# Second products of odd token tiles moved to the last stage of an attention and feed-forward kernel

## The chip, the cores and the metric

The kernel runs on one core of a Trainium2 chip. The metric is the device time of one execution in microseconds. TensorE (PE) multiplies matrices into PSUM banks; VectorE (DVE) and ScalarE (ACT) empty the banks and do element-wise work; GpSimd (POOL) does some sums and issues some DMAs; SyncE (SP) issues the other DMAs. Each engine takes its instructions in order.

## The reference

Eight batches, 12 heads, 448 positions, head width 64; the model width is 12 x 64 = 768, and the hidden width of the feed-forward part is 3072.

```python
def _attn_ref(q, k, v):
    S = q.shape[2]
    scale = 1.0 / np.sqrt(q.shape[-1])
    scores = scale * np.matmul(q, k.transpose(0, 1, 3, 2))
    attn = np.maximum(scores, 0.0) ** 2 / S
    return np.matmul(attn, v).astype(np.float32)

def _moe_ref(x, g_ln, w_ch1, w_ch2):      # x: attention's output, (8, 448, 768)
    mu = np.mean(x, axis=-1, keepdims=True)
    var = np.mean((x - mu) ** 2, axis=-1, keepdims=True)
    xn = (x - mu) / np.sqrt(var + 1e-06) * g_ln
    ch = np.maximum(xn @ w_ch1, 0.0) @ w_ch2
    return (x + ch).astype(np.float32)
```

The inputs are float32; the matrix products run in bf16 with float32 sums.

## The kernel before, in words

**Pairs and stages.** Two batches make a pair: 896 tokens, seven token tiles of 128. There are four pairs, 0 to 3. For each pair the kernel computes attention, the first product with `w_ch1` and ReLU (FFN1, into the tile `hT`, 24 row blocks of 128 hidden units by 896 tokens), and the second product with `w_ch2` (FFN2). The order on PE is written out by hand. After the first pair's start it goes: FFN2 of pair 0 with attention of pair 1 woven in, FFN1 of pair 1, FFN2 of pair 1 with attention of pair 2, FFN1 of pair 2, FFN2 of pair 2 with attention of pair 3, FFN1 of pair 3, FFN2 of pair 3 alone. The last of these is called the last stage.

**The weave.** `interleave` spreads a list of attention units over a list of FFN2 units. An attention unit is mostly a *bundle* of three score tiles (`item`, `scores`): four small matmuls on PE each (L366), a ReLU on ACT (L377) from PSUM into `attn_sb`, and a square, either on DVE (L381) or on ACT (L379). In the second and fourth pair's attention ACT squares the third tile of every bundle. A bundle may also hold a value product (`values`, 28 matmuls, L398), evicted by DVE into `xT` (L404). Score tiles and value products share a ring of three PSUM buffers of two banks each (`ps_sc`). At the last score tile of a group, `transposed` starts the key and query transposes of a later group on SP (L313, L318, L319); inputs are loaded from POOL (L159).

**FFN2 of pairs 0 and 1.** `ffn2_units` goes token tile by token tile: two column halves of 24 matmuls (128x128 by 128x384), each cut in four units of six. `finish` (L756) scales the result by the token's `rstd`, adds the residual from `xt_room` (`xtok`), and `store` sends it out on SP through one of three buffers in `o_room` (L776). Pair 1 leaves out its middle tile, `MID` = 3: `odd_out` (L789) sends that tile's 24 blocks of `hT` and its residual rows to DRAM, and its `rstd` column is kept in `odd_root`. In pair 0's stage `fold_beside` also folds the layer norm's gain and mean into `w1` on DVE (L485).

**FFN2 of pairs 2 and 3: Strassen.** `ffn2_pair` takes two token tiles at once (t and t+4). Two tiles, two halves of the hidden width and two column halves make a 2x2 by 2x2 block product, done with seven products of twelve matmuls in the place of eight. It needs sums of blocks of `hT` (`h_sums_of`, on DVE) and of `w_ch2` (`w2_sum_units`, done earlier), and sums of banks (`z`, L1130 to L1184). Pair 2 does three such pairs and its middle tile by `ffn2_mid` (48 matmuls, L1076). Pair 3 does four; the fourth is its own middle tile with the one that pair 1 sent out, read back by `odd_in` (L795) into parts of `w1` that are free by then. With `third`, `ffn2_pair` starts with products 4, 3 and 1 and puts off their last block of rows, so that the last FFN1 block (`close`) can end between them.

**FFN1 of pairs 1 to 3** is a Strassen scheme too (L903), whose weight sums are made on POOL and DVE in pair 1 (L864 to L888), kept in DRAM and read back.

Of the kernel before, what the change touches and what calls it, by code (L numbers as in the profile page):

```python
# [28 lines left out]
def kernel(  # L29
# [22 lines left out]
    nc = tc.nc  # L52
    P = 128
# [13 lines left out]
    K2 = d_ff // P  # L67
# [27 lines left out]
    odd_root = const.tile([P, 1], fp32)  # L95
# [162 lines left out]
    def transposes(b, m):  # L258
# [11 lines left out]
        if (b, m) == (0, 0):  # L270
# [5 lines left out]
            idle(32)  # L276
# [323 lines left out]
    def attention(bs, hooks):  # L600
# [25 lines left out]
        def bundle(items, at):  # L626
            for o, it in enumerate(items):
                item(*it, o == 2 and bs[0] in (by_dma, B - 2))
                if o == at:
                    product(it[0] - 1)  # L630
        units, due = [], [[]]
        for s in range(0, len(seq), 3):
            items = seq[s:s + 3]
            at = max((o for o, (n, i) in enumerate(items[:2]) if n > lo and i in (1, 2)), default=-1)
            units.append(lambda items=items, at=at: bundle(items, at))
# [149 lines left out]
    odd_kept = dram.tile([P, K2 + K1, P], bf16, name="odd_kept")  # L785
# [3 lines left out]
    def odd_out(pair):  # L789

        nc.gpsimd.dma_start(odd_kept[:, :K2], hT[pair][:, :, MID * P:(MID + 1) * P])
        nc.gpsimd.dma_start(odd_kept[:, K2:], xt_room[:, :, MID])
        odd["pair"] = pair

    def odd_in():  # L795

        t = w1[:, :KQ, :KH * P].rearrange("p c (k s) -> p c k s", s=P)
        nc.sync.dma_start(t[:, :2].rearrange("p c k s -> p c (k s)"),
                          odd_kept[:, :K2].rearrange("p (c k) s -> p c (k s)", c=2))
        nc.sync.dma_start(t[:, 2, :K1], odd_kept[:, K2:])  # L800
        odd["h"], odd["x"] = t[:, :2], t[:, 2, :K1]
# [264 lines left out]
    def ffn2_mid(pair, a, b):  # L1066

        h = hT[pair].rearrange("p (kh k) s -> p kh k s", kh=2)[:, :, :, 3 * P:4 * P]  # L1070
        s, n = room0[:, :KH], KH - 1
        a, b = a[:, :DH], b[:, :DH]

        def rows(ps, left, name, lo, hi, first=False, last=False):
            for k in range(lo, hi):
                nc.tensor.matmul(ps, left[:, k], w2_sum[name][:, k], start=(first and k == lo),  # L1076
                                 stop=(last and k == hi - 1))

        def most(*at, **kw):
            rows(*at, 0, 6, **kw)  # L1080
            yield
            rows(*at, 6, n)
        yield from most(a, h[:, 1], "t4", first=True)
        nc.vector.tensor_add(s[:, :n], h[:, 0, :n], h[:, 1, :n])
        yield
        yield from most(b, h[:, 0], "t3", first=True)
        yield
        nc.vector.tensor_add(s[:, n], h[:, 0, n], h[:, 1, n])
        h_sums_of(pair, 0, "s1")
        for half, ps, left, name, then in ((0, a, h[:, 1], "t4", "t2"), (1, b, h[:, 0], "t3", "t5")):  # L1090
            if half:
                yield
            yield from most(ps, s, then)
            rows(ps, left, name, n, KH)
            rows(ps, s, then, n, KH, last=True)
            finish(pair, 3, half, 0, K1, ps, (nc.sync, nc.sync))
            h_sums_of(pair, 0, "s2", half * KQ * 2, (half + 1) * KQ * 2)

    def ffn2_pair(pair, t, ts, two_banks, z, last, third=None):
# [3 lines left out]
        at, half = h_parts(pair, t), KH // 2  # L1103
# [20 lines left out]
        def result(ps, row, half):  # L1124
            p, u = (odd["pair"], MID) if t == MID and row else (pair, t + 4 * row)
            root = odd_root if p != pair else rstd[pair][:, u:u + 1]
# [289 lines left out]
```

## Time and profile before

| | |
|---|---|
| times of three runs | 514.38, 514.39, 516.76 us (median 514.39) |
| the profiled execution, its own time | 513.95 us |
| its span, first to last instruction | 512.2 us |
| granted TensorE clock, mean | 0.999 |
| FFN2 of pair 0 / pair 1 / pair 2 / last stage | 99.9 to 175.4 / 222.2 to 289.7 / 336.3 to 405.7 / 452.3 to 512.2 us |
| DMA moved | 76.31 MB, mean 149 GB/s |

All durations and places in time are from the one profiled execution. In rows of a timeline the columns are start, duration (both us), engine, line, operation, tiles written and read, type and count. Matmuls overlap in the pipeline, so a row of several is longer than the time to the next row.

### The profile page before, as it was taken

The numbers are of one execution on the slowest core, as the hardware profiler recorded it, in microseconds if no ns is written. First come the engines' busy times: TensorE is split into PE (matmuls) and PEld (weight loads), VectorE is DVE, ScalarE is ACT, GpSimd is POOL, SyncE is SP. The second block draws the span as 40 slices with busy tenths as digits, with TensorE's granted clock in tenths as the row PEclk, the third lists the DMA queues.
The fourth block names the chain that finished last, engine by engine and source line by source line (L and its number), as shares of the span: only waits on it lengthen the run. The fifth ranks groups of instructions, "written<-read, shape, count | busy, mean of one in ns | idle before, by whom it ended". The sixth has DMA issues, their size and how long they took to land.

```text
span 512.2 us, 11457 instructions
## 1 busy us (share of the span) xinstructions
PE 504.7 (99%) x4559; PEld 299.7 (59%) x4559; DVE 385.0 (75%) x738; ACT 310.0 (61%) x513; POOL 130.3 (25%) x182
## 2 busy tenths in 40 slices
PE   8999999999999999999999999999999999999996
PEld 6677778955555555555555555555555555556663
DVE  4885755778787798858789968858887968868663
ACT  5966776588668266657757266639979366730000
POOL 8335102012402266321101099601100022200000
PEclk9999999999999999999999999999999999999999
DMA  9999999999979994329996999304997393322222
GB/s 198 206 207 206 210 206 157 157 149 211 167 134 193 173 226 139 129 66 175 186 234 111 196 177 185 93 11 79 185 193 174 75 219 117 94 77 63 63 61 61
DMA packets 124486, 76.31 MB, mean 149 GB/s; under 512 B 80562, under 2 KB 120498, under 8 KB 124434
## 3 DMA queue, kind: packets, MB, share of 16 engines
q1 hardware_dynamic: 93730, 41.38, 39.5%
q0 software_dynamic: 28544, 30.91, 37.4%
q10 hardware_dynamic: 2160, 3.31, 2.8%
q8 instruction: 35, 0.57, 0.5%
q14 instruction: 17, 0.14, 0.1%
HBM read 64.69 MB, written 17.89 MB: 161 GB/s over the span
## 4 chain that ended last, share of the span: by engine, by line
PE 95%; ACT 2%; DVE 2%; issue 0%; ACTq 0%
PE m_ps L903 28%; PE o_ps L745 19%; PE o_ps L1114 11%; PE m_ps L1114 8%; PE h_ps L686 8%; PE sc_ps L366 7%; PE av_ps L398 6%; PE h_ps L731 2%; ACT early L377 2%; PE h_ps L713 2%; PE o_ps L1076 2%; PE tr_ps L250 1%; PE idle_ps L236 1%; PE sum_ps L431 0%; DVE w L485 0%; ACT attn_sb L377 0%
## 5 line engine op out<-in xcount | busy, mean ns | idle before, releaser
L377 ACT ACTIVATE attn_sb<-sc_ps 128x896 bf16<-128x896 f32 (+4 forms) x150 | 126.3, 903 | 37.5 <-PE sc_ps L366 32.4
L907 ACT ACTIVATE hT_sb<-m_ps 128x448 bf16<-128x448 f32 x144 | 78.2, 543 | 52.1 <-PE m_ps L903 49.3
L745 PE MATMUL o_ps<-w,hT_sb 128*128 128x384 bf16 x624 | 107.6, 326 | 0.0
L745 PEld LDWEIGHTS <-hT_sb 128*128 128x128 bf16 x624 | 58.4, 98 | 46.0 <-issue 9.9
L381 DVE TENSOR_TENSOR attn_sb<-attn_sb 128x896 bf16<-128x896 bf16 x98 | 60.0, 622 | 25.0 <-ACT attn_sb L377 24.4
L686 PE MATMUL h_ps<-x_room,w 128*128 128x192 bf16 (+2 forms) x384 | 43.9, 263 | 0.0
L1114 PEld LDWEIGHTS <-hT_sb 128*128 128x128 bf16 x312 | 29.8, 98 | 22.0 <-issue 3.0
L985 DVE TENSOR_TENSOR m_ps<-x_room,m_ps 128x448 f32<-128x448 f32 x36 | 22.6, 628 | 21.6 <-ACT hT_sb L907 21.5
L686 PEld LDWEIGHTS <-w 128*128 128x128 bf16 x384 | 33.8, 97 | 6.9 <-issue 1.4
L903 PEld LDWEIGHTS <-w 128*128 128x128 bf16 x246 | 24.0, 97 | 22.8
L1114 PEld LDWEIGHTS <-x_room 128*128 128x128 bf16 x252 | 24.2, 98 | 17.3 <-issue 1.6
L404 DVE TENSOR_SCALAR xT_sb<-av_ps 128x896 bf16<-128x896 f32 (+2 forms) x30 | 27.0, 900 | 9.2 <-PE av_ps L398 8.9
L967 ACT COPY x_room<-m_ps 128x448 f32<-128x448 f32 x36 | 19.1, 531 | 21.2 <-PE m_ps L903 20.5
L903 PEld LDWEIGHTS <-w_sum 128*128 128x128 bf16 x210 | 20.5, 98 | 19.3 <-DVE w_sum L879 0.4
L159 POOL DMA_DIRECT2D k_sb<-in_k_dram x15 | 10.7, 713 | 79.6 <-DMA kT_sb<-k_sb 57.2
L159 POOL DMA_DIRECT2D v_sb<-in_v_dram x20 | 14.2, 710 | 58.6 <-PE sc_ps L366 44.2
L903 PE MATMUL m_ps<-x_sum,w 128*128 128x448 bf16 x120 | 29.1, 352 | 0.0
L663 DVE BATCH_NORM_STATS2 stats<-xtok_sb 128x6 f32<-128x384 bf16 x56 | 28.3, 547 | 0.9 <-DMA xtok_sb<-xT_sb 0.9
L366 PE MATMUL sc_ps<-qT_sb,kT_sb 64*64 64x448 bf16 x392 | 28.1, 358 | 0.2 <-ACT x_room L481 0.2
L485 DVE SCALAR_TENSOR_TENSOR w<-w,g_sb,x_room 128x512 bf16<-128x512 bf16 x36 | 25.6, 738 | 3.0 <-ACT x_room L481 3.0
L379 ACT ACTIVATE attn_sb<-attn_sb 128x896 bf16<-128x896 bf16 x28 | 26.6, 950 | 0.9
L398 PE MATMUL av_ps<-attn_sb,v_sb 64*64 64x448 bf16 (+2 forms) x532 | 26.1, 330 | 0.0
(196 smaller groups left out, 867.6 us busy)
## 6 DMA issues: line engine op xcount, KB each, us to landing
out_dram<-o_room SPq DMA_DIRECT2D x108, 96.0 KB, 2.5
w<-in_moe_w_ch_dram POOLq DMA_DIRECT2D x12, 384.0 KB, 14.1
w<-in_moe_w_ch_dram POOLq DMA_DIRECT2D x4, 1152.0 KB, 20.1
q_sb<-in_q_dram POOLq DMA_DIRECT2D x20, 224.0 KB, 5.9
v_sb<-in_v_dram POOLq DMA_DIRECT2D x20, 224.0 KB, 6.2
k_sb<-in_k_dram POOLq DMA_DIRECT2D x15, 224.0 KB, 5.3
kept<-room SPq DMA_DIRECT2D x4, 480.0 KB, 2.6
kept<-w_sum SPq DMA_DIRECT2D x16, 96.0 KB, 1.8
```

The costliest lines, as they stand in the source:

```text
L366: nc.tensor.matmul(ps[cols, r, o * w:(o + 1) * w], g["k"](i)[rows, cols], g["q"](i, r)[rows, blk[0]:sum(blk), cols], start=True, stop=True)
L377: nc.scalar.activation(a, ps[:, :, :len(slots) * w], ACTF.Relu)
L379: nc.scalar.activation(a, a, ACTF.Square)
L381: nc.vector.tensor_mul(a, a, a)
L398: nc.tensor.matmul(ps[cols, hh, :w], v_sb[rows, pr, j * D:(j + 1) * D], g["attn"][i][rows, r, :], start=(j == 0), stop=(j == J - 1))
L404: nc.vector.tensor_scalar_mul(x, ps[:, :, :w], score_scale)
L663: nc.vector.bn_stats(stats[:, n], xtok[pair][:, n * G:(n + 1) * G, t, :])
L686: nc.tensor.matmul(ps[:, :w + more], w1[:, c, ni * P:(ni + 1) * P], xc[b][:, c, s.start:s.stop + more], start=(c == 0), stop=(c == K1 - 1))
L745: nc.tensor.matmul(ps[:, :DH], hT[pair][:, ki, t * P:(t + 1) * P], w2[:, ki, cols], start=(o == 0), stop=(o == K2 - 1))
L903: nc.tensor.matmul(ps, *at, start=(first and c == 0), stop=(c == KQ - 1), skip_group_check=not first)
L907: nc.scalar.activation(hT[pair][:, n + KH * row, half * S:(half + 1) * S], ps, ACTF.Relu)
L1114: nc.tensor.matmul(ps, x[:, ki], y[ki] if isinstance(y, list) else y[:, ki], start=(first and ki == 0), stop=(ki == KH - 1), skip_group_ch ...
```

## The change

Pairs 0 and 2 now treat their middle token tile as pair 1 did: `odd_out` sends it to DRAM, one DRAM tile for each pair, and the last stage reads all three back. It pairs pair 3's middle tile with pair 1's, as before, and pair 0's with pair 2's as a fifth Strassen pair. The room for the third tile is `xT` of pair 3. `ffn2_mid` is gone, and pair 2's second product now starts with the `third` form. Further edits go along: two idle matmuls fewer at the start, the fold's steps placed at other units of the now shorter list in pair 0's stage, and in the fourth pair's attention ACT squares the third tile in two of three bundles, DVE in the others.

```diff
-    odd_root = const.tile([P, 1], fp32)
+    odd_root = const.tile([P, B // 2], fp32)
...
-            idle(32)
+            idle(30)
...
-        for i, n in ((2, 1), (3, 2), (4, 16), (5, 28)):
+        for i, n in ((2, 1), (3, 2), (4, 15), (5, 25)):
             more.setdefault(n, []).append(lambda i=i: fold_mean(i))
         for o in range(4 * K1):
-            more.setdefault(4 + o * 2, []).append(lambda o=o: fold_into(2 + o // K1, o % K1))
+            more.setdefault(3 + o * 42 // 24, []).append(lambda o=o: fold_into(2 + o // K1, o % K1))
+        more.setdefault(24, []).append(lambda: odd_out(0))
...
+        squares = {by_dma: (0, 1, 2), B - 2: (0, 1)}.get(bs[0], ())
+
-        def bundle(items, at):
+        def bundle(items, at, turn):
             for o, it in enumerate(items):
-                item(*it, o == 2 and bs[0] in (by_dma, B - 2))
+                item(*it, o == 2 and turn in squares)
...
     def odd_out(pair):
 
-        nc.gpsimd.dma_start(odd_kept[:, :K2], hT[pair][:, :, MID * P:(MID + 1) * P])
-        nc.gpsimd.dma_start(odd_kept[:, K2:], xt_room[:, :, MID])
-        odd["pair"] = pair
+        nc.gpsimd.dma_start(odd_kept[pair][:, :K2], hT[pair][:, :, MID * P:(MID + 1) * P])
+        nc.gpsimd.dma_start(odd_kept[pair][:, K2:], xt_room[:, :, MID])
 
     def odd_in():
 
-        t = w1[:, :KQ, :KH * P].rearrange("p c (k s) -> p c k s", s=P)
-        nc.sync.dma_start(t[:, :2].rearrange("p c k s -> p c (k s)"),
-                          odd_kept[:, :K2].rearrange("p (c k) s -> p c (k s)", c=2))
-        nc.sync.dma_start(t[:, 2, :K1], odd_kept[:, K2:])
-        odd["h"], odd["x"] = t[:, :2], t[:, 2, :K1]
+        x = xT[B // 2 - 1].rearrange("p c s -> p (c s)")[:, :(K2 + K1) * P].rearrange("p (c s) -> p c s", s=P)
+        for pair, room in ((1, w1[:, :KQ, :KH * P]), (0, w1[:, KQ:, KH * P:]), (2, None)):
+            if room is None:
+                to, odd[pair] = x[:, :K2].rearrange("p (c k) s -> p c k s", c=2), {"x": x[:, K2:]}
+            else:
+                t = room.rearrange("p c (k s) -> p c k s", s=P)
+                to, odd[pair] = t[:, :2], {"x": t[:, 2, :K1]}
+            odd[pair]["h"] = to
+            nc.sync.dma_start(to.rearrange("p c k s -> p c (k s)"),
+                              odd_kept[pair][:, :K2].rearrange("p (c k) s -> p c (k s)", c=2))
+            nc.sync.dma_start(odd[pair]["x"], odd_kept[pair][:, K2:])
...
-        two = [h[:, :, :, t], odd["h"] if t == MID else h[:, :, :, t + 4]]
+        if t > MID:
+            two = [odd[0]["h"], odd[2]["h"]]
+        else:
+            two = [h[:, :, :, t], odd[1]["h"] if t == MID else h[:, :, :, t + 4]]
...
-    def ffn2_mid(pair, a, b):
...
     def ffn2_pair(pair, t, ts, two_banks, z, last, third=None):
...
+        at, half, s1 = h_parts(pair, t), KH // 2, h_sum["s1"]
+        if third is not None and pair < B // 2 - 1:
+            h_sum["s1"] = room0[:, :KH]
...
+            p, u = (pair, t + 4 * row) if t < MID else (((pair, 1), (0, 2))[t - MID][row], MID)
+            root = odd_root[:, p:p + 1] if p != pair else rstd[pair][:, u:u + 1]
+            x = odd[p]["x"] if p != pair else xtok[pair][:, :, u]
...
-        order = [t for t in range(NT) if pair != 1 or t != MID]
+        order = [t for t in range(NT) if t != MID]
+        then = dict(zip(order, order[1:] + [MID]))
...
     def strassen_units(pair, mm, banks, third=None):
         def all_of():
             end = pair == pairs - 1
-            if not end:
-                yield from ffn2_mid(pair, *mm)
-            for t in range(MID + end):
+            ts = MID + 2 * end
+            for t in range(ts):
...
-        return [lambda: next(g)] * 4, [lambda: next(g)] * (4 + 3 * 14), g
+        return [lambda: next(g)] * 4, [lambda: next(g)] * (9 + 2 * 14), g
...
-            head, units, _ = strassen_units(pair, mm, lambda t: mm[::-1] if t % 2 else mm)
+            third = ps_m.tile([P, 512], fp32, tag="m", name="m_ps")
+            head, units, _ = strassen_units(pair, mm, lambda t: mm[::-1] if t % 2 else mm, third)
...
             stage["close"]()
-            if pair == 1:
-                odd_out(pair)
+            odd_out(pair)
+            if last:
+                units.pop(0)()
+                nc.vector.tensor_copy(odd_root[:, pair:pair + 1], rstd[pair][:, MID:MID + 1])
```

More of the change, by code (lines that the diff above doesn't have):

```diff
@@ L784 @@
     kept = dram.tile([P, KH, 5 * KQ, P], bf16, name="kept")
-    odd_kept = dram.tile([P, K2 + K1, P], bf16, name="odd_kept")
+    odd_kept = [dram.tile([P, K2 + K1, P], bf16, name=f"odd_kept{p}") for p in range(B // 2 - 1)]
     MID = NT // 2
@@ L1124, in result @@
         def result(ps, row, half):
-            p, u = (odd["pair"], MID) if t == MID and row else (pair, t + 4 * row)
-            root = odd_root if p != pair else rstd[pair][:, u:u + 1]
-            x = odd["x"] if p != pair else xtok[pair][:, :, u]
+            p, u = (pair, t + 4 * row) if t < MID else (((pair, 1), (0, 2))[t - MID][row], MID)
+            root = odd_root[:, p:p + 1] if p != pair else rstd[pair][:, u:u + 1]
+            x = odd[p]["x"] if p != pair else xtok[pair][:, :, u]
             o = next_out()
@@ L1299, in all_of @@
             end = pair == pairs - 1
-            if not end:
-                yield from ffn2_mid(pair, *mm)
-            for t in range(MID + end):
-                yield from ffn2_pair(pair, t, MID + end, banks(t), zs[t % 2], end and t == MID,
+            ts = MID + 2 * end
+            for t in range(ts):
+                yield from ffn2_pair(pair, t, ts, banks(t), zs[t % 2], end and t == ts - 1,
                                      third if t == 0 else None)
@@ L1342 @@
             stage["close"]()
-            if pair == 1:
-                odd_out(pair)
+            odd_out(pair)
+            if last:
+                units.pop(0)()
+                nc.vector.tensor_copy(odd_root[:, pair:pair + 1], rstd[pair][:, MID:MID + 1])
             narrow.close()
```

33 lines of the change are left out of this document (2 added, 31 removed).

## The prediction

> **What bounds the kernel now.** I read the busy times first, then the chain that ended last, then busy times by stage, then the timelines of the three engines in the one stage that gets shorter with most attention work beside it.
>
> The page's first part and the head of its chain:
>
> ```profile
> PE 504.7 (99%) x4559; PEld 299.7 (59%) x4559; DVE 385.0 (75%) x738; ACT 310.0 (61%) x513; POOL 130.3 (25%) x182
> ...
> PE 95%; ACT 2%; DVE 2%; issue 0%; ACTq 0%
> ```
>
> TensorE (PE) is the path nearly everywhere, so a matmul taken away counts in full unless another engine is then too slow for the shorter stage. The busy times by stage (second product of pair 0, of pair 1, of pair 2, last stage):
>
> ```profile
> 99.90:175.40 75.50, 75.29 (x690) 41.56 (x688) 58.55 (x108) 53.17 (x69) 16.23 (x22) 1.00 1.04 171
> ...
> 222.20:289.70 67.50, 67.50 (x633) 36.25 (x631) 55.11 (x101) 38.98 (x53) 10.75 (x14) 1.00 0.99 166
> ...
> 336.30:405.70 69.40, 69.40 (x644) 37.63 (x642) 54.76 (x86) 51.36 (x63) 5.03 (x7) 1.00 0.69 127
> ...
> 452.30:512.20 59.90, 55.70 (x342) 33.24 (x340) 37.78 (x60) 3.54 (x7) 0.00 (x0) 0.99 0.26 70
> ```
>
> The columns are stretch, length, PE, weight loads, DVE, ACT, POOL, granted clock, DMA share, GB/s. PE is full in each; in the last stage it ends about 4 us before the span does. ACT (51.36 of 69.40) and DVE (54.76) have room in the pair-2 stage, but on average only. Timelines of PE and ACT there:
>
> ```profile
> 347.95 0.76 PE L366 MATMUL sc_ps<-qT_sb,kT_sb 64*64 64x448 bf16 x12
> 348.65 2.12 PE L1114 MATMUL o_ps<-w,hT_sb 128*128 128x384 bf16 x12
> 350.70 0.76 PE L366 MATMUL sc_ps<-qT_sb,kT_sb 64*64 64x448 bf16 x12
> ...
> 348.43 2.54 ACT L377 ACTIVATE attn_sb<-sc_ps 128x896 bf16<-128x896 f32 x3
> 351.01 0.95 ACT L379 ACTIVATE attn_sb<-attn_sb 128x896 bf16<-128x896 bf16 x1
> 351.87 2.51 ACT L377 ACTIVATE attn_sb<-sc_ps 128x896 bf16<-128x896 f32 x3
> ```
>
> A bundle is three score tiles (0.69 us of PE) and, after twelve matmuls of the second product, comes every 2.75 us (347.95 to 350.70). ACT takes 3.44 us for it (348.43 to 351.87: three ReLUs, one square). So after twelve matmuls ACT falls behind; after eighteen (about 3.7 us) or with a value product (1.42 us more of PE) it catches up.
>
> **PE work.** A 384-column matmul costs 0.1625 us (the chain has 40.96 us for 252 of them in the last stage). Pair 0 loses one token tile: 48 matmuls, -7.80 us. Pair 2 loses its middle tile, also 48 (L1076: 3.58+3.09+1.24 us in the chain, which includes overlap): -7.80. The last stage gains one Strassen pair: seven products of twelve, 84 matmuls, +13.65. Sum -1.95 us. At the start 30 instead of 32 idle matmuls: 3.42/32 = 0.107 us each, -0.21; the transposes behind need q's cast, which ends at 4.23 us, and 4.61-0.21 = 4.40 is still later. I count -0.2. Together -2.15 us. Nothing else of PE's order is new: pair 2 now starts as the last stage does (4, 3, 1 of a first pair around the last FFN1 block), and that start shows no idle PE from 452.3 to 459.3.
>
> **Last stage.** One pair costs DVE 9.2 us per 14.0 of PE (470 to 484), so the fifth fits. Its loads are three times what is loaded now on SP, 2.9 MB. Store and load of the one tile that goes this way now, from the list of DMA issues (KB, us to landing):
>
> ```profile
> odd_kept<-hT_sb POOLq DMA_DIRECT2D x1, 768.0 KB, 8.2
> ...
> w<-odd_kept SPq DMA_DIRECT2D x1, 768.0 KB, 4.3
> ```
>
> Three of the second kind one after another are about 13 us from 450 us; the first use, sums for the fourth pair, is two and a half pairs (over 30 us) later. Six issues of 0.40 to 0.46 us stand ahead of the first output store on SP, which went out at 461.88: hidden, 0. Were they late, the price would be the lateness itself, at most some us; nothing speaks for that. The end (last product, eviction, store) is unchanged.
>
> **The new stores.** Each is 2.3 us of POOL issue (1.46+0.84 at 226.2) and 8 us of DMA. For pair 0 it is queued on POOL ahead of two FFN1 weight sums and of a key and a query load (138.47, 139.21) whose transpose starts at 165: 26 us of cover, 0. Pair 0's output stores fall by 384 KB meanwhile. For pair 2 POOL was idle from 328 to 354.73, so no instruction waits; the transfer runs from about 342 to 350, just before the transposes of 351.13. The root copies are one tiny DVE instruction each (0.16, like the reciprocal): hidden.
>
> The 768 KB store took almost twice as long as the load of the same bytes, beside other traffic; its source pieces are 256 bytes, the load's 3 KB. By the row, pair 2's copy is over at about 350 and costs 0. [...]
>
> **Pair 0's stage.** 67.7 us instead of 75.5. DVE 58.55 less two evictions (1.2) plus a copy is 57.5, 85%; ACT 53.2, 79%. Pair 1's stage of 67.50 holds 55.11 of DVE without idle PE, though with ACT at 38.98. Of the fourteen bundles only five now follow twelve matmuls, each with a longer one before or a value product after it. The one old stall (0.21 at 140.4, behind a fold's copy) may go or double. I take +0.2, ends -0.2 and +1.
>
> **Pair 2's stage.** 61.6 instead of 69.4. DVE: four squares come from ACT (+2.5), the middle tile goes (-5.2 with its sums and two evictions), the first pair's sums in the last stage's form come (+3.0), one copy +0.2: 55.3, or 90% instead of 79%. ACT: 51.36-3.8 = 47.6; but between the first and the last bundle PE needs 28 units of six, 27.3, fourteen rounds less one of scores, 9.0, five value products, 7.1, and about 1.2 of switching, 44.6 us, and ACT 13 x 2.55 + 9 x 0.87 + 2 x 0.4 = 41.8: 94%. Every bundle but one now follows twelve matmuls. Bundles 1 and 2 both have a square on ACT. With bundle 1 at 0, ACT begins at 0.48 and is free at 3.92; bundle 2's third ReLU ends at 6.46; bundle 3 comes at 5.50 and its third tile, at 5.96, needs that buffer (three in the ring): 0.5 us of idle PE. Then each value product sits in the ring between the bundle's tiles, and a late ACT holds the last tile 0.2 to 0.3 us, five times: 1.2. One late DVE eviction of a value product, 0.5. The upper sum is 2.2; the lower end is 0, as the same patterns cost the old stage 0.07 twice at most. A stall also lets ACT catch up, so they don't all add: I take 1.15.
>
> **Sum.** -2.15+0.2+1.15 = -0.8. The profiled execution took 513.95 (span 512.2), 0.44 under the median of 514.39; from it 513.15, from the median 513.6.
>
> **Rivals.** *Vector engine as the bound in pair 2's stage (slower).* DVE is in order; in the old stage it stood 7.3 us waiting for ReLUs with work queued behind. If half of that (3.7) now comes through to PE, because late squares hold the value products and late evictions the banks, on top of 1.4 us at the ring, PE idles 5.1 us: -2.15+0.2+5.1 = +3.1, 517.5. It decides once DVE is two bundles (5.5 us) late. For: 90%; three squares in every third bundle. Against: 55.11 of 67.50 cost pair 1 nothing, and a product's banks have twelve matmuls of slack.
>
> *Late transposed keys and queries.* For the third group of that stage:
>
> ```profile
> 368.50 1.44 SPq L313 DMA_TRANSPOSE kT_sb<-k_sb  x1
> 370.03 3.55 SPq L318 DMA_TRANSPOSE qT_sb<-q_sb  x1
> 373.63 2.03 SPq L319 DMA_TRANSPOSE qT_sb<-q_sb  x1
> ```
>
> Released by scores at 366.84, landing 6.0 us after 373.63, so 12.8 us; PE wanted them at 380.08. Now 2.75+4.17+4.70-0.23 = 11.4 us lie between the same points: 1.4 us of idle PE on top of the sum, 515.0. The first group has more room: its last transpose lands at about 356.9, 6.2 us after its scores (350.70), and is wanted at 7.4 at the earliest. Against: SP stood behind six output stores first, which may fall otherwise.
>
> *Nothing is given back:* 512.2. *Or the old stalls go too,* with up to 0.6 more: 511.6.
>
> [...]
>
> **Chances.** Forecast 0.46 (its own range 512.2 to 515.2); late transposes 0.18; vector engine 0.23; nothing given back 0.07; stalls go 0.04; slow start 0.02. Half a per cent (2.57 us) is about what a measurement of this kernel can tell from no change. Faster than 511.8: 0.04. Slower than 517.0: the vector engine's 0.23. Within: 0.73. The range 512.0 to 517.5 leaves out the upper half of the vector case and the last stalls.
>
> **What would show it.** Right: the last stage 13.7 us longer on PE with no gap; the two shortened stages at 67.9 and 62.8; idle PE in pair 2's stage ended by ReLUs, first at bundle 3. Wrong: a fourth or fifth last-stage pair waiting for loads; gaps above 2 us ended by DVE or by a transpose; a pair-2 stage above 65 or below 61.6.

## The result, and the profile after

The changed kernel is slower: 520.6 us, median of six runs (519.07 to 522.38), beside 514.84 for six runs of the kernel before (514.26 to 516.76) on the same chip. The ratio is 1.0106, 95% interval 1.0075 to 1.0138. The forecast was 513.6 with a range up to 517.5. The profiled execution took 522.07 us, span 520.3; it is one of the longer ones.

The page's busy times and the head of its chain, for the changed kernel:

```profile
PE 504.3 (97%) x4545; PEld 299.3 (58%) x4545; DVE 394.3 (76%) x755; ACT 306.2 (59%) x510; POOL 135.1 (26%) x186
...
PE 79%; DMA 11%; ACT 4%; DVE 2%; issue 2%; POOL 1%; SPq 1%; ACTq 0%; DVEq 0%; POOLq 0%
```

The count of matmuls fell by 14 (4559 to 4545), as planned. But PE's busy time fell only by 0.4 us (504.7 before), and the chain, which had 95% of PE and no DMA in its head line, now runs through DMAs for 11% of the span. Work went away; waits came. The busy times by stage say where: second product of pair 0, of pair 1, FFN1 of pair 2, second product of pair 2, last stage (columns as in the prediction).

```profile
99.70:170.30 70.60, 68.06 (x642) 37.04 (x641) 58.33 (x106) 52.47 (x69) 18.76 (x24) 1.00 1.20 191
...
217.10:284.50 67.40, 67.40 (x631) 36.27 (x630) 55.12 (x101) 38.93 (x53) 10.76 (x14) 1.00 0.98 168
284.50:334.46 49.96, 46.97 (x248) 23.95 (x246) 36.49 (x74) 30.90 (x58) 33.62 (x40) 1.00 0.64 130
334.46:400.10 65.64, 62.72 (x596) 33.86 (x594) 54.85 (x87) 47.62 (x59) 7.27 (x9) 1.00 0.75 136
...
446.66:520.30 73.64, 69.38 (x426) 41.46 (x424) 47.03 (x76) 4.03 (x9) 0.00 (x0) 1.00 0.33 94
```

In the shortened stages and in FFN1 of pair 2, PE's busy time is 2.5 to 3.0 us below the length (in the last stage the difference is its end). FFN1 of pair 2 has an unchanged program and stood in no step of the forecast; in the kernel before PE was busy in all of it:

```profile
289.70:336.30 46.60, 46.60 (x247) 24.02 (x246) 36.55 (x73) 30.86 (x58) 33.63 (x40) 1.00 0.70 142
```
From here on a stage runs from its first second-product or FFN1 matmul in the trace to the first of the next, which gives this balance (us):

| stage | before | forecast | after | miss |
|---|---|---|---|---|
| start | 99.77 | 99.57 | 99.61 | 0.0 |
| second product, pair 0 | 75.54 | 67.94 | 70.55 | +2.6 |
| FFN1, pair 1 | 46.77 | 46.77 | 46.77 | 0 |
| second product, pair 1 | 67.43 | 67.43 | 67.42 | 0 |
| FFN1, pair 2 | 46.67 | 46.67 | 49.94 | +3.3 |
| second product, pair 2 | 69.40 | 62.75 | 65.66 | +2.9 |
| FFN1, pair 3 | 46.53 | 46.53 | 46.54 | 0 |
| last stage, PE | 55.90 | 69.55 | 69.55 | 0.0 |
| end | 4.17 | 4.17 | 4.25 | +0.1 |
| span | 512.2 | 511.4 | 520.3 | +8.9 |

PE's waits in the changed kernel, longest first (sum, times, longest); 1.1 us at the start (L236) are in both kernels:

```profile
PE m_ps L911 <- DMA w_sum<-kept: 1.7, 1, 1.7
PE sc_ps L366 <- DMA qT_sb<-q_sb: 1.4, 2, 1.2
PE m_ps L911 <- DVE x_room L977: 1.3, 1, 1.3
PE av_ps L398 <- ACT x_room L481: 1.1, 1, 1.1
...
PE sc_ps L366 <- ACT attn_sb L377: 1.1, 4, 0.4
PE sc_ps L366 <- ACT x_room L481: 1.0, 1, 1.0
PE sc_ps L366 <- DVE xT_sb L404: 0.6, 2, 0.3
...
PE o_ps L1094 <- DVE o_room L1110: 0.4, 1, 0.4
```

L911 is FFN1 of pair 2. L481, the copy of a fold's mean on ACT, belongs to pair 0's stage. The waits for `qT_sb` and `o_room`, and most of those for L377, lie in pair 2's stage. The kernel before has no wait of PE in FFN1 of pair 2 or in pair 2's stage. The waits add up to less than the loss: in pair 2's stage PE is also "busy" for 62.72 us where 61.6 us of matmuls remain. It was busy for 62.41 us in a later run with five waits there and for 61.85 in one with two. That the waits make it longer is the author's guess; no run tests it alone.

### The profile page after: what moved, and what is told of

The parts are those of the page before. It is cut to its first block, busy times and chain, and to the rows that moved or that the text cites. A ratio compares the mean times of both kernels' runs of the same rounds, so it can differ in the third digit from the quotient of the medians.

```text
span 520.3 us, 11474 instructions
## 1 busy us (share of the span) xinstructions
PE 504.3 (97%) x4545; PEld 299.3 (58%) x4545; DVE 394.3 (76%) x755; ACT 306.2 (59%) x510; POOL 135.1 (26%) x186
## 2 busy tenths in 40 slices
DMA packets 125735, 80.25 MB, mean 154 GB/s; under 512 B 80690, under 2 KB 120882, under 8 KB 125682
## 4 chain that ended last, share of the span: by engine, by line
PE 79%; DMA 11%; ACT 4%; DVE 2%; issue 2%; POOL 1%; SPq 1%; ACTq 0%; DVEq 0%; POOLq 0%
PE m_ps L911 26%; PE o_ps L748 17%; PE m_ps L1094 11%; PE o_ps L1094 7%; PE h_ps L689 6%; DMA xtok_sb<-xT_sb 5%; PE sc_ps L366 5%; PE av_ps L398 5%; ACT attn_sb L377 3%; DMA w<-in_moe_w_ch_dram 3%; DMA v_sb<-in_v_dram 2%; PE h_ps L716 1%; DMA out_dram<-o_room 1%; DVE o_room L1110 1%; DMA qT_sb<-q_sb 1%
## 5 line engine op out<-in xcount | busy, mean ns | idle before, releaser
L377 ACT ACTIVATE attn_sb<-sc_ps 128x896 bf16<-128x896 f32 (+4 forms) x150 | 126.0, 902 | 37.1 <-PE sc_ps L366 33.6
L748 PE MATMUL o_ps<-w,hT_sb 128*128 128x384 bf16 x576 | 99.7, 327 | 0.0
L748 PEld LDWEIGHTS <-hT_sb 128*128 128x128 bf16 x576 | 53.8, 98 | 43.0 <-issue 9.8
L381 DVE TENSOR_TENSOR attn_sb<-attn_sb 128x896 bf16<-128x896 bf16 x102 | 63.3, 631 | 19.7 <-ACT attn_sb L377 18.8
L1094 PEld LDWEIGHTS <-hT_sb 128*128 128x128 bf16 x312 | 29.9, 98 | 21.4 <-issue 2.1
L993 DVE TENSOR_TENSOR m_ps<-x_room,m_ps 128x448 f32<-128x448 f32 x36 | 22.6, 629 | 21.8 <-ACT hT_sb L915 21.7
L911 PEld LDWEIGHTS <-w 128*128 128x128 bf16 x246 | 24.0, 97 | 24.2 <-issue 1.6
L1094 PEld LDWEIGHTS <-x_room 128*128 128x128 bf16 x276 | 26.5, 98 | 19.6 <-issue 2.6
L911 PEld LDWEIGHTS <-w_sum 128*128 128x128 bf16 x210 | 20.4, 98 | 21.2 <-DMA w_sum<-kept 2.1
L911 PE MATMUL m_ps<-x_sum,w 128*128 128x448 bf16 x120 | 29.1, 353 | 1.3 <-DVE x_room L977 1.3
L485 DVE SCALAR_TENSOR_TENSOR w<-w,g_sb,x_room 128x512 bf16<-128x512 bf16 x36 | 25.9, 754 | 3.0 <-ACT x_room L481 3.0
L1094 PE MATMUL m_ps<-w,x_room 128*128 128x384 bf16 x156 | 27.2, 327 | 0.0
L1094 PE MATMUL o_ps<-w,hT_sb 128*128 128x384 bf16 x144 | 25.9, 327 | 0.0
```

The lines of the kernel that those rows point to most:

```text
L377: nc.scalar.activation(a, ps[:, :, :len(slots) * w], ACTF.Relu)
L381: nc.vector.tensor_mul(a, a, a)
L485: nc.vector.scalar_tensor_tensor(w, w, g_sb[:, c:c + 1], fold["means"][i % 2].rearrange("p (h n) -> p h n", h=2), op0=ALU.mult, op1=ALU.add)
L748: nc.tensor.matmul(ps[:, :DH], hT[pair][:, ki, t * P:(t + 1) * P], w2[:, ki, cols], start=(o == 0), stop=(o == K2 - 1))
L911: nc.tensor.matmul(ps, *at, start=(first and c == 0), stop=(c == KQ - 1), skip_group_check=not first)
L1094: nc.tensor.matmul(ps, x[:, ki], y[ki] if isinstance(y, list) else y[:, ki], start=(first and ki == 0), stop=(ki == KH - 1), skip_group_ch ...
```

## Experiments: where each loss sits

**The changed kernel again** (no edit).

> The changed kernel once more, to see which of its idle times return. If the lost time belongs to the order of the work: the stage of pair 0's second product (between the last matmul of the first stage and the first of the second FFN1) again 70 to 71 us, the second FFN1 stage (third pair, program unchanged) again 50 us instead of 46.6, the stage of pair 2's second product again 65 to 66 us. If the second FFN1 stage lost its 3.3 us to transfers that landed late in that one execution: about 46.7 us here, and a span near 517.

520.04 us. Pair 0's stage 69.94, FFN1 of pair 2 48.93, pair 2's stage 64.50: 2.0, 2.3 and 1.8 us above the forecast in place of 2.6, 3.3 and 2.9. All three losses return, smaller, and FFN1 of pair 1 took 47.44. So they belong to the kernel, with a part that differs between executions.

**Only pair 0's tile moves.**

```diff
-            ts = MID + 2 * end
+            ts = MID + 2 * end
+            if not end:
+                yield from ffn2_mid(pair, *mm)
...
-            odd_out(pair)
+            if pair == 1:
+                odd_out(pair)
```

> Only pair 0's odd tile moves; pair 2's stage is that of the kernel before. The fifth pair of the last stage takes pair 1's data for its second row and does not store that row. The TensorE has 48 matmuls (7.80 us) more than in the changed kernel. Theory that each shortened stage loses time by itself (pair 0's about 2.9 us, pair 2's about 4.0): pair 0's stage 70 to 71 us, pair 2's 69.4 us as before, time 520.6 + 7.8 - 4.0 = 524.4. Rival, that the loss in pair 2's stage is caused by the moved data of pair 0 or by later traffic: pair 2's stage stays 3 to 4 us above its matmuls, 73 us, time 528.

525.57 us, ratio 1.0193 (1.0157 to 1.023). Pair 0's stage 69.52, pair 2's 69.51 as before, FFN1 of pair 2 48.55. The rival (73 us in pair 2's stage) falls. The start of the profiled execution took 102.49 us, 2.9 more than usual; see the last section.

**Only pair 2's tile moves.**

```diff
-        order = [t for t in range(NT) if t != MID]
+        order = [t for t in range(NT) if pair != 1 or t != MID]
...
-        more.setdefault(24, []).append(lambda: odd_out(0))
...
-            idle(30)
+            idle(32)
```

> Only pair 2's odd tile moves; pair 0's stage is that of the kernel before, with its folds and its token transposes. The fifth pair of the last stage takes pair 1's data for its first row and does not store that row. Theory that each shortened stage loses by itself: pair 0's stage 75.5 us as before, pair 2's 65.6 us, time 520.6 + 7.8 - 2.9 = 525.5, and 522.2 if the 3.3 us of the second FFN1 stage come from pair 0's shortened stage too. Rival, that the loss in pair 2's stage depends on what pair 0 left: pair 2's stage 62 us and time 522 or less with the second FFN1 stage at 50.

521.63 us, ratio 1.0154 (1.009 to 1.0218). Its end is 1.84 us shorter than the changed kernel's (2.41 in place of 4.25), since the last row is not stored, so it compares as 523.5. Pair 0's stage 75.54, FFN1 of pair 2 46.67, pair 2's 64.79. So pair 2's stage loses by itself, and the loss in FFN1 of pair 2 came with pair 0's part of the change; two unshortened stages lie between.

**No transfers of the two tiles.**

```diff
-        for pair, room in ((1, w1[:, :KQ, :KH * P]), (0, w1[:, KQ:, KH * P:]), (2, None)):
+        for pair, room in ((1, w1[:, :KQ, :KH * P]),):
...
-        more.setdefault(24, []).append(lambda: odd_out(0))
...
-            odd_out(pair)
+            if pair == 1:
+                odd_out(pair)
```

> The changed kernel without the stores and loads of pair 0's and pair 2's odd tiles; the fifth pair of the last stage reads other data at hand and those two tiles of the output are not stored. Matmuls and vector work stay. Theory that the shortened stages run out of cover (late key and query transposes, output stores, rings): stages of 70 to 71, 50 and 65 to 66 us stay, time 520 to 521. Rival, that the added 5.8 MB of transfers crowd out the transposes and fetches: second FFN1 stage 46.7, pair 2's stage 62 to 63, time 514 to 516.

516.66 us, but its end is 2.64 us shorter for the same reason (1.61), so 519.3 compares with 520.0 to 520.6. Stages 71.07, 48.62 and 64.03: all three losses stay. The added bytes (the page has 80.25 MB in place of 76.31, so 3.9 MB and not the 5.8 of the expectation) are not the cause; about 1 us is theirs at most, by the times.

## Experiments: FFN1 of pair 2

In this stage DVE's moments of the fourth token tile (`stats`) wait for the last of the token transposes, issued 22.16 us into the stage; the sum of banks behind them (L977) then holds up PE. One line of DVE's waits in this stage of the changed kernel:

```profile
DVE stats L666 <- DMA xtok_sb<-xT_sb: 3.5, 1, 3.5
```

DVE wants the transpose at 28.55 us of the stage. Before, it landed at 28.35, 0.2 us ahead; in the changed kernel at 32.08. What the transposes meet on the way is in the DMA view of 308 to 313 us (23.6 to 28.6 us of the stage; 40 slices of 0.125 us):

```profile
GB/s 25 25 31 57 111 102 168 74 123 338 82 102 80 18 0 0 0 0 16 0 8 8 8 18 14 195 78 96 72 88 201 231 367 223 386 336 322 295 197 129
...
q8 instruction: 1, 0.02, 1.4%
```

Queue q8 is one of the two that the page calls instruction queues. It makes 35 fetches of 16 KB in the kernel before and in the changed one, 126 matmuls apart on average, and a fetch changes its place with the number of TensorE's instructions ahead of it (table below), so it is taken for the fetch of TensorE's code. 4,545 matmuls, each with its weight load, are about 260 instructions a fetch (an estimate from these counts). Its fetch begins at 309.2, and from 309.6 to 311.1 next to nothing moves. In the kernel before the fetch fell 12.1 us into the stage; without 48 matmuls ahead of it, it falls at 24.9. The same stretch of the kernel before (313.1 to 318.1 us) has no fetch of q8 and two of q14, the other instruction queue, and is down for about 0.75 us only:

```profile
GB/s 48 72 92 74 84 254 62 135 152 123 88 72 43 418 311 301 337 332 389 381 147 229 179 195 213 259 14 14 29 12 18 18 266 393 442 98 262 344 461 416
...
q14 instruction: 2, 0.02, 0.8%
```

No wait of PE in the list above is put down to a fetch, but the transfers beside this one all but stood still from 309.6 to 311.1 us.

PE's wait of 1.7 us for `w_sum<-kept`, a weight sum that is read back, is the same stop at another transfer: it ends 28.5 us into the stage. It adds nothing to the loss, since DVE's moments after the late transpose run 3.28 us later than before, which is already all of the 3.3 us.

To move the fetch alone, 32, 64 or 96 TensorE instructions of 16 columns were put at the start of the changed kernel, and 64, 80 or 88 at the start of the kernel before:

```diff
             idle(30)
+            for _ in range(64):
+                nc.tensor.matmul(idle_ps[:, 0, :16], ones, ones[:, :16], start=True, stop=True)
```

> The changed kernel with 64 more TensorE instructions of 16 columns behind the idle products at the start; nothing else differs. Theory: what the second FFN1 stage (third pair) loses comes from where the 16 KB fetches of TensorE's code fall. In the kernel before, one falls 12.1 us into that stage, in the changed kernel, which has 48 matmuls fewer ahead of it, 24.7 us into it, onto the token transposes that are needed at 28.1 us. 64 more instructions put it back at about 12 us, and the stage takes 46.7 to 47.2 us in place of 48.6 to 50; the time is 520.6 - 2.5 and what the 64 instructions cost at the start (1 to 4 us). Rival, that the stage loses because the one before it is shorter (other transfers pushed into it): the stage stays at 48.6 to 50.

> The kernel before with the same 64 instructions at the start and nothing of the change. Theory of the code fetches: they now fall where the changed kernel has them, 24 to 25 us into the second FFN1 stage, and that stage takes 48.5 to 50 us in place of 46.67, all other stages within 0.3 us of before. Rival, that the shortened stage ahead is the cause: 46.67 as before.

> The kernel before with 80 in place of 64 more TensorE instructions at the start, nothing of the change. With 64, the second code fetch of the second FFN1 stage fell 27.8 us into it, after the token transposes had landed, and the stage stayed at 46.67. 16 more should move it about 3 us forward, to 24 to 25.5 us, where the changed kernel has it. Theory of the code fetches: the stage takes 48 to 50 us in the kernel before as well. Rival, that the shortened stage of pair 0 is needed for the loss: 46.67.

> The changed kernel with 32 in place of 64 more TensorE instructions at the start. The code fetch that falls 24.4 to 25.9 us into the second FFN1 stage should fall at 18 to 19 us, before the transposes that count are moving. If that fetch is what makes them late, the stage takes 46.7 to 47.3 us, as with 64 (47.26); if the changed kernel's transposes are late without it, 48.5 to 50.

> The changed kernel with 96 more instructions at the start: the code fetches of the second FFN1 stage should fall at about 6 and 30 us, again clear of the transposes of 22 to 28 us. With the fetch as the cause 46.7 to 47.3 us; without 48.5 to 50.

> The kernel before with 88 more instructions at the start, nothing of the change. With 80 the fetch fell at 25.3 us, the last transpose landed at 28.55 us, and the vector engine needed it at 28.55, so that nothing was lost. With 88 the fetch should fall at about 23.8 us, so that more of the transfer lies behind it. If the fetch alone makes the transposes late, the stage takes 47.5 us or more; if the kernel before keeps 46.67, the fetch is not enough by itself and something in the changed kernel's stage ahead is needed too.

All kernels with that stage's order, by the places of TensorE's code fetches in it (us into the stage), one profiled execution in each row:

| kernel | fetches at | last transpose lands | stage |
|---|---|---|---|
| before | 12.1, 37.0 | 28.35 | 46.67 |
| only pair 2 | 12.9, 37.1 | 28.09 | 46.67 |
| before + 64 | 0.2, 27.8 | 27.73 | 46.67 |
| before + 80 | 25.3, 45.3 | 28.55 | 46.67 |
| before + 88 | 22.5, 45.3 | 30.56 | 48.47 |
| after + 96 | 3.0, 29.1 | 29.36 | 47.21 |
| after + 64 | 11.1, 34.2 | 29.40 | 47.26 |
| after + 32 | 14.9, 40.5 | 29.50 | 47.35 |
| no transfers | 0.5, 24.4, 47.8 | 30.77 | 48.62 |
| only pair 0 | 24.9, 47.7 | 30.70 | 48.55 |
| stores, idle 32 (below) | 25.3, 46.7 | 30.41 | 48.26 |
| after, first profile | 24.9, 49.1 | 32.08 | 49.94 |
| after, again | 25.9, 48.0 | 31.08 | 48.93 |

Six runs with a fetch between 22 and 26 us have a late landing and a stage of 48.3 us or more; one (before + 80) just got through, with the landing 0.2 us later than before. None of the six without such a fetch is above 47.35. The kernel before, with nothing of the change, loses 1.8 us when the fetch is moved to 22.5. PE's waits in that stage of the kernel before with 88 more instructions:

```profile
PE m_ps L905 <- DVE x_room L971: 1.2, 1, 1.2
PE m_ps L905 <- DMA w_sum<-kept: 0.3, 1, 0.3
```

The runs with 32, 96, 80 and 88 were executed once each (521.39, 523.02, 516.16 and 518.48 us).

So the place of the fetch is the larger part, about 1 to 2.7 us of the 1.6 to 3.3. The rival has a part too: with the fetch out of the way the changed kernel still lands 1.0 us or more later than the kernel before, and loses 0.5 to 0.7 us. Where that rest comes from is open. Two expectations failed: before + 64 put the fetch at 27.8 instead of 24 to 25, and before + 80, in the right place, lost nothing.

The 64 instructions did not make the changed kernel faster (520.19 us, ratio 1.0093, 1.006 to 1.0127). In its profile the start took 100.67 us, 1.1 more, and FFN1 of pair 1 48.00, 1.2 more; other fetches move too, but none of these was tested. In the kernel before (516.39, ratio 1.0042, 1.002 to 1.0064) the start took 104.13 us (see the last section), and pair 2's stage 70.99 instead of 69.40 with one new wait, shown here; with 88 it took 70.27:

```profile
PE o_ps L1116 <- DVE o_room L1132: 1.4, 1, 1.4
```

**Earlier transposes, the folds, the squares.** If the landing is what counts, an earlier issue must cure it wherever the fetch falls. The edits for pair 0's and pair 2's stages are in the same run.

```diff
-        for i, n in ((2, 1), (3, 2), (4, 15), (5, 25)):
+        for i, n in ((2, 1), (3, 2), (4, 16), (5, 28)):
...
-        squares = {by_dma: (0, 1, 2), B - 2: (0, 1)}.get(bs[0], ())
+        squares = {by_dma: (0, 1, 2), B - 2: (0, 1, 2)}.get(bs[0], ())
...
-        if n < K1:
-            tokens_part(2, 3, NT, (n,))
+        if n < KQ:
+            tokens_part(2, 3, NT, (2 * n, 2 * n + 1))
```

> The changed kernel with three edits, each in a stage of its own. (1) Pair 0's stage: the fold means of the last two columns return to units 16 and 28; if the 1.11 us wait at 25 us of the stage belongs to the fold mean at unit 15, it goes and the stage falls from 69.9 to about 68.6; if it belongs to the shortened stage, it stays somewhere. (2) Second FFN1 stage: the token transposes are issued in three steps instead of six; with them landed by 20 us the late code fetch meets nothing and the stage takes 46.7; if the transposes are not the cause, 48.6 to 50. (3) Pair 2's stage: the square of each bundle's last scores on the scalar engine in all bundles, as before; the ring wait of 0.40 us at 15.5 us goes or moves to the scalar engine's side, the wait of 0.34 us for the vector engine at 22.5 us goes; the stage stays above 63 if the late transposes and pipeline refills make up the rest. Sum if all three hold: 520.6 - 1.3 - 2.5 - 0.5 = 516.3.

517.12 us, ratio 1.005 (1.0035 to 1.0066). FFN1 of pair 2 took 46.62 us, without a wait, with a fetch at 22.6; the three further kernels with this edit and the last one below took 46.62 as well. So the late transposes are the cause of the loss, whatever delays them. Pair 0's stage fell to 68.76, as expected: the wait of 1.11 us went with the fold mean's place. The wait is gone in the four other profiles with the means at 16 and 28 too. Pair 2's stage rose to 65.05 with all squares on ACT, with a new wait of 0.89 us for ACT: that expectation failed.

## Experiments: pair 2's stage and pair 0's

**Half of each output tile on the GpSimd queue, and 32 idle products.**

```diff
-            store(p, u, slice(half * DH, (half + 1) * DH), o, (nc.sync, nc.scalar if last else nc.sync),
+            store(p, u, slice(half * DH, (half + 1) * DH), o,
+                  (nc.sync, nc.scalar if last else nc.sync if pair == B // 2 - 1 else nc.gpsimd),
...
-            idle(30)
+            idle(32)
```

> The changed kernel with two edits. (1) 32 idle products at the start as before, in place of 30; if the wait of 0.3 to 1.5 us at 4 to 5 us of pair 0's stage comes from starting 0.2 us earlier, it goes. (2) Pair 2's stage sends half of each output tile on the GpSimd queue instead of the sync queue; if the late transposes of the third and fourth group and the output tile that is not free come from the sync queue's backlog, these waits (0.2 to 0.3, 0.2 to 1.2 and 0.4 us) go and the stage falls from 64.5-65.7 to about 63.5. If the transfers are slow for another reason, they stay.

519.22 us, ratio 1.0091 (1.0061 to 1.0121). Pair 2's stage took 64.50, with waits of 0.27 us for transposes and 0.26 us for an output tile: no less than in the second profile of the changed kernel. The waits for transposes and output tiles there are 1.85 us in its first profile, 0.28 in its second, 1.16 with 96 more instructions (stage 64.98), and none with 32 or 64 more or without the transfers, where the stage took 64.03 each time. So SP's backlog is not shown to be the cause; these waits differ between executions and kernels, and under them lie 64.0 us. The wait at the head of pair 0's stage was 0.23 us, but it was as short with 30 idle products in other runs, so the expectation's first part isn't shown either.

**Folds and transposes alone; then one ACT square in three bundles; then GpSimd for six subtractions.**

```diff
-        squares = {by_dma: (0, 1, 2), B - 2: (0, 1)}.get(bs[0], ())
+        squares = {by_dma: (0, 1, 2), B - 2: (0,)}.get(bs[0], ())
...
         elif name == "s6":
-            nc.vector.tensor_sub(a[1, 0], a[1, 0], a[0, 0])
+            (nc.gpsimd if pair == B // 2 - 2 else nc.vector).tensor_sub(a[1, 0], a[1, 0], a[0, 0])
...
-            nc.vector.tensor_sub(a[0, 1], a[0, 1], a[1, 1])
+            (nc.gpsimd if pair == B // 2 - 2 else nc.vector).tensor_sub(a[0, 1], a[0, 1], a[1, 1])
```

> The changed kernel with the fold means at units 16 and 28 and the token transposes of the third pair in three steps; squares in pair 2's stage as in the changed kernel. Theory: pair 0's stage 68.7, second FFN1 stage 46.6, pair 2's stage 64.0 to 64.5 (0.5 to 1 us below the 65.05 with all squares on the scalar engine), time 516.2. Rival, that the 0.89 us wait at 20.7 us of pair 2's stage came with the earlier transposes and not with the squares: 65 again, time 517.1.

> As the run with folds and transposes alone, but in pair 2's stage one of three bundles, not two, squares its last scores on the scalar engine (0.95 us each there, 0.62 us on the vector engine). If the waits at 15.5, 27.3, 34.5 and 46.7 us (0.40, 0.16, 0.16, 0.5) come from the scalar engine, which has 3.49 us for a bundle of 2.77 us on TensorE, they shrink and the stage takes 63.3 or less. If the vector engine (54.9 of 65 us busy) is the one that lacks room, its waits grow and the stage takes 64.5 or more.

> As the run before it, and in pair 2's stage the six subtractions of 0.95 us that make the left factors of the sixth and seventh products run on GpSimd, which has 7 us of work there. Theory that the ring, fed by the scalar and the vector engine together, sets the loss: with both relieved the waits go and the stage takes 62 to 63 us, time 514.5 to 515.5. Rival, that GpSimd's own 3 to 4 us for each subtraction come too late or slow the vector engine down beside it: 64.5 or more, with a wait for GpSimd ahead of the sixth products.

Folds and transposes alone: 519.43 us, ratio 1.0079 (1.005 to 1.0109), and not 516.2; pair 2's stage 64.55, as expected, but pair 0's took 72.72: a wait of 2.2 us at its head and what followed it (last section). One square: 517.63, ratio 1.0049 (1.0027 to 1.0071); pair 2's stage 64.51, the same. Two of the four waits for ACT shrank from 0.16 to 0.1 and below, those of 0.40 and 0.47 stayed, since the square of the first bundle still stands ahead of them. DVE's wait stayed at 0.3 and 0.7 us was a late transpose, so neither branch of the expectation came as written. GpSimd: 521.38, ratio 1.0122 (1.0105 to 1.0139), pair 2's stage 68.66: worse, though not with the wait that the rival named; PE waited for DVE's squares and evictions (last section).

**ACT's squares left out.**

```diff
-            nc.scalar.activation(a, a, ACTF.Square)
+            if groups[n][0] < 6:
+                nc.scalar.activation(a, a, ACTF.Square)
...
-        more = {0: [lambda: statistics(0, 0), lambda: roots(0, 0, 1)]}
+        more = {2: [lambda: statistics(0, 0), lambda: roots(0, 0, 1)]}
```

> The run with folds and transposes alone, with two edits in stages of their own. (1) Pair 2's stage: the squares on the scalar engine (0.95 us in two of three bundles) are left out, nothing replaces them; the output is then not the reference's there. If the scalar engine holds up the ring of score tiles, the waits at 15.5, 27.3, 34.5 and 46.7 us go and the stage takes 62.0 to 63.0 us (0.34 at 22.5 for the vector engine and up to 0.7 for late transposes may stay); if these waits only mark where TensorE has too little work of its own, they stay near 64. (2) Pair 0's stage: the moments of the first token tile, which wait for the token transposes, come at the third unit instead of the first. If the wait of 0.2 to 2.2 us at 4 to 6 us of the stage comes from the vector engine standing in front of that transfer, it goes and the stage takes 68.3 us; if it is the fold's own work, it stays.

PE's waits in pair 2's stage: first of the changed kernel with 32 more instructions, which has no DMA wait there, then of this run.

```profile
PE sc_ps L368 <- ACT attn_sb L379: 1.3, 4, 0.5
PE sc_ps L368 <- DVE xT_sb L406: 0.3, 1, 0.3
```

```profile
PE sc_ps L366 <- DMA qT_sb<-q_sb: 1.0, 1, 1.0
PE sc_ps L366 <- DVE xT_sb L405: 0.4, 1, 0.4
```

The run took 518.09 us (one execution). The four waits for ACT are gone, PE's busy time is 61.85 us in place of 62.41, and the stage takes 63.28, of which 1.05 is a late transpose. ACT's squares make the ring late: shown. Without the DMA wait about 62.2 us would remain, so the squares cost about 1.8 of the 64.0 us (an estimate). In pair 0's stage the later moments changed nothing: a wait of 2.0 us stayed at its head. There ACT stands, in order, at the root of the first token tile, which needs DVE's moments, which need the first token transposes; with the moments later in the program it stands there just the same, ahead of the second fold mean. DVE could begin the moments at 102.3 us in the first profile of the changed kernel and at 102.5 here, at 100.1 in the kernel before. These transposes are late already in their issue on SP, which lasts longer in the changed kernel (the kernel before, then the changed one):

```profile
84.29 12.17 SPq L652 DMA_TRANSPOSE xtok_sb<-xT_sb  x1
```

```profile
84.12 14.52 SPq L655 DMA_TRANSPOSE xtok_sb<-xT_sb  x1
```

In both, DVE's moments begin 3.6 to 3.7 us after the issue ends. In the other profiles with pair 0's stage shortened the wait at its head is 0.2 to 2.2 us; why the issue lasts longer is open.

No version tried beats the kernel before, and the best stages seen (start 99.6; 68.76, 46.77, 67.43, 46.62, 64.03, 46.53, 69.55; end 4.2) add up to a span of 513.5, still above 512.2.

## Why the prediction was wrong, step by step

Three steps failed. FFN1 of pair 2, behind a shortened stage, had no term and lost 3.3 us. Pair 0's stage was judged by busy shares and lost 2.8 us in place of 0.2. Pair 2's stage had the right mechanism with a term that was too small, 4.1 us in place of 1.15.

- *PE work, last stage, the loads of the tiles, the start:* right. The last stage grew by 13.65 without a gap, the start fell by 0.16, and PE lost 2 x 48 matmuls.
- *The new stores, 0:* right in size. Leaving out all new transfers gains at most about 1 us. Pair 2's store landed after 6.95 us, not later than the 8.2 of the row, and the first group's transposes kept no one waiting in either profile of the changed kernel.
- *Pair 0's stage, +0.2 (ends -0.2 and +1), measured +2.8, so a miss of 2.6.* The step judged the stage by busy shares (85%, 79%), which came out about right (58.33 us of DVE for 57.5, 52.47 of ACT for 53.2). The loss is nearly all in three single waits: 1.11 us behind a fold mean that had been moved by one unit into a bundle that needed its ring buffer, 0.34 at the ring late in the stage, and 0.96 at its head behind the first token transposes. Putting the fold mean back took the first away; for the other two no run shows the cause by a change. The move of the folds was in the diff and was not priced; the only price was for the old stall "behind a fold's copy", which "may go or double".
- *FFN1 of pair 2, no term, measured +3.3.* This is the step that was missing. The stage had a transfer that landed 0.2 us before it was needed, a margin that the busy times do not show; 48 matmuls fewer ahead of it moved a code fetch onto that transfer (1 to 2.7 us). The other 0.5 to 0.7 us come with the transposes' later landing in the changed kernel, whose cause is open.
- *Pair 2's stage, +1.15 (ends 0 and 2.2), measured +4.1 in the first profile, a miss of 2.9.* The mechanism was right, and so were the busy times (54.85 us of DVE for 55.3, 47.62 of ACT for 47.6): the first wait came at the third bundle, 0.40 us for 0.5 forecast, then the late eviction, 0.34 for 0.5, then the value products' bundles, 0.16, 0.16 and 0.5 for 0.2 to 0.3 each. The size was the upper end and a little more: with these waits alone the stage takes 64.0 us, that is 2.4 above its 61.6 us of matmuls. The waits add up to 1.6; the other 0.8 is PE's longer busy time (62.41 us), for which the sum had no term. Taking half of the upper sum, because ACT catches up in a stall, was too little. The rest, 0 to 1.6 us, is transfers.
- *Rivals.* Late keys and queries came: 0.19 us at the third group (1.4 priced) and 1.23 at the fourth in the first profile, 0.28 in the second. The vector engine did not become the bound: with one more square in three bundles on DVE the stage was as long (64.51). The slow start of the chances did not come with the two idle products fewer: the start was 99.6 us with 30 and 99.8 with 32.
- *Chances.* Slower by over 0.5% had 0.23 on one mechanism. It came by three others at once, two above the ends of their ranges and one without a term. Of the signs named, the last stage without a gap and the first wait for a ReLU at the third bundle came, and so did a sign of being wrong, a pair-2 stage above 65 us (65.66; the second time 64.50). Every price had been looked for inside the two shortened stages; what moves in the stages behind them had none.

## What to carry to other kernels

Before work is taken out of a full engine's stream, list for every stage behind it, changed or not, how long each transfer lands before it is wanted; a margin of 0.2 us was lost here to a shift three stages ahead, and an earlier issue cured it. In a weave, price the in-order engine that frees the ring bundle by bundle (here 3.4 us of ACT against 2.75 us of PE) and take the upper sum. Here 48 matmuls fewer moved a code fetch from 12.1 to 24.9 us of an unchanged stage, so a change of a per cent should be tried at more than one place of the fetches before its worth is believed.

## What the hardware showed that was not expected

**Transfers stood still behind a code fetch.** For about 1.5 us next to nothing moves behind TensorE's 16 KB fetch in the view above; the same fetch in the kernel before falls where it costs nothing. It isn't so behind every fetch. During the loads at the start of the kernel before the core kept on moving about 205 GB/s around the one at 29.9 us and about 211 around the one at 47.1, in views of 5 us each. What decides it was not tested; DMA transposes were on their way in the stage that lost.

**A square on DVE beside a subtraction on GpSimd.** Beside one of the six subtractions on GpSimd, a bf16 square on DVE took 4.02 us in place of 0.62 (DVE, then GpSimd):

```profile
362.42 4.02 DVE L381 TENSOR_TENSOR attn_sb<-attn_sb 128x896 bf16<-128x896 bf16 x1
```

```profile
362.84 3.11 POOL L1075 TENSOR_TENSOR hT_sb<-hT_sb 128x1536 bf16<-128x1536 bf16 x1
```

This square ends 0.49 us after the subtraction; its row begins 0.42 us ahead of the subtraction's, so which of the two began first can't be read from the starts. Two rows of two squares each, from 341.00 and from 355.30 us, took 4.79 and 3.12 us, with subtractions from 341.66 to 344.76 and from 354.26 to 357.39. The stage's 37 squares on DVE took 32.9 us, beside 22.2 in the run that differs in GpSimd's subtractions alone. What makes them longer was not tested.

**Half the clock after a wait of two microseconds.** After the wait of 2.2 us at the head of pair 0's stage (folds and transposes alone), the granted clock in that stage was (the column after POOL):

```profile
106.40:107.40 1.00, 0.90 (x10) 0.36 (x10) 0.72 (x3) 1.00 (x2) 0.00 (x0) 0.97 1.15 107
107.40:110.70 3.30, 3.30 (x12) 1.52 (x11) 2.85 (x5) 2.74 (x4) 0.70 (x1) 0.50 1.47 87
```

The half clock lasted about 3.4 us, 3.3 of them in the second row, which costs 1.7 us on top of the wait (an estimate from these rows). The same came after the 2.0 us of the run without ACT's squares, whose clock was 0.57 in the mean from 106 to 110 us, again about 3.4 us at half. It did not come after 1.66 us in FFN1 of the changed kernel (1.00 in that stage), 1.77 there with only pair 0's tile moved, or 1.47 without the transfers; the mean clocks of those last two executions are 0.998 and 1.000, where 3.4 us at half take 0.003 off the mean. Those of the two with the half clock are 0.995 and 0.996.

**Some starts are longer.** The record of the granted clock begins, at full, 6.03 us after the span's start in the kernel before and 5.37 in the changed one, whose starts took 99.77 and 99.61 us. With only pair 0's tile moved, an edit that doesn't touch the start, the start took 102.49 us, and PE had 96 matmuls in the first 10 us where the changed kernel had 129. It took 104.13 us in the kernel before with 64 more instructions and 104.15 in the changed kernel with 32 more; there eight score products (64x192) took 0.53 us at 7.14 us, and 0.36 at 6.08 without these instructions. What decides it was not tested.
